# P times V for eight key tiles behind every second block, the down projection behind the others

## The chip, the cores and the metric

The kernel runs on one core of one Trainium2 chip. The metric is the device time of one execution in microseconds (us), the median of several runs. The core has five engines with queues of their own: TensorE (PE, its weight loads are listed as PEld), VectorE (DVE), ScalarE (ACT), GpSimd (POOL) and SyncE (SP, which here only issues DMAs). Each works through its queue in order and waits there for semaphores of the others.

## The reference

One sequence of S = 2048 rows with D = 576 features, H = 32 heads of 18, F = 4608. All in float32.

```python
xn = layernorm(x)
# attention
q, k, v = split(xn @ wqkv)                       # 32 heads of 18
p = softmax(q @ k.T * 18 ** -0.5)                # full, 2048 x 2048 for each head
s = concat(p @ v) @ wo
# gated block
gate, up = xn @ W_gate, xn @ W_up                # 2048 x 4608
b = (gate * (gate > 0) * up) @ W_down
out = x + s * silu(b)
```

## The kernel before, in words

A first stage (to about 200 us) makes the normalised rows, their transpose, and q, k, v. The main stage is a sequence of **144 blocks**, k = 0 to 143: 4 groups of 512 rows of x, and in each 36 tiles of 128 of the 4608 features. `up(k)` multiplies one such feature tile (gate on PE rows 0 to 63, up on rows 64 to 127, two matmuls side by side), three products each since every operand is held as a high and a low part. `emit_unit(k)` (from L868) writes a block. Into its 27 pairs of gate and up matmuls (`pg`) it deals two kinds of attention matmuls, which use the same half arrays:

- `psx`, the scores of 128 keys against 512 queries, whose exponential ACT writes to a buffer `p` (L97, tile from the pool `pp`: one buffer holds one key tile for two heads and 1024 queries);
- `pm`, scores whose row maxima DVE takes (L272) for the next pair of heads.

From block 16 on, each of the 16 pairs of heads takes eight blocks: 16 `psx` and 16 `pm` in each block, so four key tiles. I call this stretch of a block its **row run**. Behind it, before the change, stand

- `attend()`, P times V: for each finished key tile four matmuls of 32 columns side by side (`po`; the chip shows two instructions for each float32 matmul). After 16 key tiles `finish` has ACT evict the result (`ot`) and leaves a task `rest_` for DVE: transpose (`tq`), reciprocal (`rc`), scaling, transpose back (`on`);
- in even blocks the tasks (`run_tasks`: `rest_` and `max_rows`, which collects the maxima with a reduction and a transpose, `nm` and `nt`) and then `down(k - 1)`, the down projection of two feature tiles: eight results `py` of six matmuls each, each added to the rows `y` by DVE (L725).

Scores, maxima and `py` share one pool of PSUM banks, `psS` with five buffers used in turn (`shared(...)`), so the result that is made as the fifth after another waits until that one has been read. All matmuls, all DVE operations and all of POOL's (`vec`, `gp`) stay in the order in which they are written.

`gate_step` turns one finished tile of 128 rows of `y` into silu: ACT writes a tanh to `e` (one buffer, L736), POOL scales `e` and multiplies `y` by it, and POOL sends `y` to DRAM. It is called once in a block, at the ninth pair of the row run, while a group's four tiles are waiting. POOL also splits raw weights into high and low parts (`split_up`: `gw` from `rg`; `split_down`: `dw` from `rd`).

## Time and profile before

| what | us |
|---|---|
| median of 3 runs (2610.35 to 2611.09) | 2610.72 |
| the profiled execution's own time | 2611.43 |
| its span, first to last instruction | 2609.7 |
| PE busy, DVE busy | 2590.9, 1900.1 |
| ACT busy, POOL busy | 1383.3, 1197.8 |

The span and what lies around it (1.7 us) make up the profiled execution's time, which is 0.7 us over the median. In the timeline, a row is a start, a length, the engine, the line, the operation with its tiles, and a count where equal neighbours were merged; in brackets stands how long the engine had been idle and what released it.

### The profile page before, as it was taken

The numbers are of one execution on the slowest core, as the hardware profiler recorded it, in microseconds if no ns is written. First come the engines' busy times: TensorE is split into PE (matmuls) and PEld (weight loads), VectorE is DVE, ScalarE is ACT, GpSimd is POOL, SyncE is SP. The second block draws the span as 40 slices with busy tenths as digits, with TensorE's granted clock in tenths as the row PEclk, the third lists the DMA queues.
The fourth block names the chain that finished last, engine by engine and source line by source line (L and its number), as shares of the span: only waits on it lengthen the run. The fifth ranks groups of instructions, "written<-read, shape, count | busy, mean of one in ns | idle before, by whom it ended". The sixth has DMA issues, their size and how long they took to land.

```text
span 2609.7 us, 54494 instructions
## 1 busy us (share of the span) xinstructions
PE 2590.9 (99%) x21788; PEld 2035.6 (78%) x21788; DVE 1900.1 (73%) x3145; ACT 1383.3 (53%) x2594; POOL 1197.8 (46%) x971
## 2 busy tenths in 40 slices
PE   8999999999999999999999999999999999999999
PEld 7898887777777777777777777777777777777778
DVE  5335678788878788787887787887777878778235
ACT  2321135556665556555666555555556655555642
POOL 5246764344464434443455444444346444434554
PEclk9999999999999999999999999999999999999999
DMA  7867422222542322232363222222253232222245
GB/s 246 274 211 162 104 74 69 70 73 74 116 121 57 82 65 70 58 79 64 80 150 88 67 69 72 65 73 68 71 128 105 73 75 60 76 58 62 67 121 183
DMA packets 263806, 253.11 MB, mean 97 GB/s; under 512 B 27648, under 2 KB 208896, under 8 KB 263552
## 3 DMA queue, kind: packets, MB, share of 16 engines
q1 hardware_dynamic: 255808, 222.48, 32.9%
q0 software_dynamic: 7744, 27.14, 3.1%
q8 instruction: 172, 2.82, 0.5%
q14 instruction: 82, 0.67, 0.1%
HBM read 203.01 MB, written 46.01 MB: 95 GB/s over the span
## 4 chain that ended last, share of the span: by engine, by line
PE 97%; DMA 1%; POOL 1%; DVE 1%; issue 0%; ACT 0%; SPq 0%; POOLq 0%; DVEq 0%; ACTq 0%
PE pg L68 32%; PE po L68 19%; PE py L68 18%; PE pm L68 11%; PE psx L68 9%; PE pq L68 4%; PE pv L68 2%; PE pw L68 2%; DMA rg<-in_B_W_up_dram 0%; PE tps L76 0%; POOL wv L85 0%; DMA xt<-in_A_x_dram 0%; DMA ro<-od 0%; SPq L97 0%; DMA y<-gd 0%
## 5 line engine op out<-in xcount | busy, mean ns | idle before, releaser
L272 DVE TENSOR_REDUCE mx<-pm 128x1 f32<-128x512 f32 x2048 | 1363.9, 689 | 268.8 <-PE pm L68 148.9
L97 ACT ACTIVATE p<-psx 128x512 f32<-128x512 f32 x2048 | 1097.9, 603 | 583.0 <-PE psx L68 541.5
L68 PE MATMUL pg<-x,gw 64*128 64x512 f32 x7560 | 1372.8, 394 | 2.3 <-POOL gw L85 1.8
L68 PEld LDWEIGHTS pg<-x,gw 64*128 64x128 f32 x7560 | 1033.5, 186 | 85.9 <-issue 3.7
L85 POOL TENSOR_TENSOR hh<-h,hh 128x512 fp32r<-128x512 f32 x144 | 184.3, 1280 | 812.7 <-ACT hh L97 790.7
L68 PEld LDWEIGHTS py<-dw,hh 128*128 128x128 f32 x3456 | 460.1, 188 | 56.1 <-issue 31.8
L68 PE MATMUL py<-dw,hh 128*128 128x288 f32 x3456 | 476.8, 297 | 0.0
L68 PE MATMUL po<-p,va 128*32 128x512 f32 x4096 | 465.9, 595 | 0.0
L725 DVE TENSOR_TENSOR y<-py,y 128x288 f32<-128x288 f32 x544 | 244.3, 454 | 225.9 <-PE py L68 225.8
L85 POOL TENSOR_TENSOR gw<-rg,gw 128x1152 fp32r<-128x1152 f32 x144 | 385.9, 2680 | 11.6
L68 PEld LDWEIGHTS po<-p,va 128*32 128x32 f32 x4096 | 119.8, 109 | 276.2 <-issue 265.4
L85 POOL CAST dw<-rd 128x576 fp32r<-128x576 f32 x144 | 95.8, 665 | 387.7 <-PE py L68 382.1
L68 PE MATMUL psx<-qT,kq 56*128 56x512 f32 x608 | 229.8, 392 | 0.0
L68 PE MATMUL pm<-kq,qT 54*128 54x512 f32 x608 | 228.7, 398 | 0.1
L85 POOL TENSOR_TENSOR dw<-rd,dw 128x576 fp32r<-128x576 f32 x144 | 206.3, 1433 | 11.6
L97 ACT ACTIVATE hh<-h 128x512 fp32r<-128x512 f32 x144 | 90.8, 630 | 220.7 <-DVE h L696 220.7
L68 PE MATMUL psx<-kq,kA 56*128 56x512 f32 x512 | 195.4, 393 | 0.3 <-DVE h L696 0.2
L68 PE MATMUL pm<-kq 54*128 54x512 f32 x512 | 195.3, 402 | 0.0
L68 PE MATMUL psx<-kq 56*128 56x512 f32 x512 | 194.2, 392 | 0.0
L68 PE MATMUL pm<-kA,kq 54*128 54x512 f32 x512 | 193.6, 400 | 0.1
L85 POOL CAST gw<-rg 128x1152 fp32r<-128x1152 f32 x144 | 165.4, 1149 | 0.0
L68 PE MATMUL pm<-kA,qT 54*128 54x512 f32 x416 | 159.4, 402 | 0.0
(92 smaller groups left out, 2180.5 us busy)
## 6 DMA issues: line engine op xcount, KB each, us to landing
rg<-in_B_W_gate_dram SPq DMA_DIRECT2D x144, 288.0 KB
rg<-in_B_W_up_dram SPq DMA_DIRECT2D x144, 288.0 KB
rd<-in_B_W_down_dram SPq DMA_DIRECT2D x144, 288.0 KB
x<-xTd SPq DMA_DIRECT2D x72, 256.0 KB
qd<-hh POOLq DMA_DIRECT2D x16, 512.0 KB, 5.0
kd<-hh POOLq DMA_DIRECT2D x16, 512.0 KB, 6.1
xTd<-x SPq DMA_DIRECT2D x16, 512.0 KB
kq<-kd SPq DMA_DIRECT2D x210, 36.0 KB
```

Source lines behind the costliest of these rows:

```text
L68: return tc.keep_in_program_order(nc.tensor.matmul(*args, **kw))
L85: return lambda *args, **kw: tc.keep_in_program_order(op(*args, **kw))
L97: i = op(*args, **kw)
L272: vec(nc.vector.tensor_reduce(mx[:, h, b, j, c : c + 1], ps, axis=AX.X, op=ALU.max))
L725: vec(nc.vector.tensor_tensor(ys[j][:, cs], ps, ys[j][:, cs], ALU.add))
```

## The change

The row run stays. Behind an odd block now stand all eight key tiles of two blocks, and behind an even block the down projection alone. `max_rows` runs behind each block in which it falls due (these are odd ones), `rest_` from a list of its own (`outs`) in the even blocks, ahead of the down projection. For eight buffers `p`, memory comes from seven places: one buffer of raw weights (`wr`) in place of two, blocks 2 to 15 borrow `p` buffers for theirs; `hh` has three buffers in place of four and `h` one in place of two, with the ReLU written into it; `yp` five in place of six; the buffer of the last output weights and those of the last stage's rows are taken from `wr` and from a weight buffer; DMA scratch shrinks. `gate_step` is called twice in a block, at pairs 9 and 25.

```diff
-    wr = pool(early, "wr", 2)
+    wr = pool(early, "wr", 1)
...
     def load_up(k):
         if k < len(units):
             f = units[k][1]
-            rgs[k] = wr.tile([P, KC, P], F32, name="rg")
+            if 1 < k < N1:
+                rgs[k] = as_rg(pp.tile([P, 4, 512], F32, name="p"))
+            else:
+                rgs[k] = wr.tile([P, KC, P], F32, name="rg")
...
-    pp = pool(mid, "pp", 4, "right")
-    w4 = pool(mid, "w4", 1, "right")
+    pp = pool(mid, "pp", 8, "right")
     wl = pool(mid, "wl", 2, "right")
-    yp = pool(mid, "yp", 6, "right")
+    yp = pool(mid, "yp", 5, "right")
...
-        r = hp.tile([P, 512], F32, name="r", bufs=1)
-        ac.activation(r, ps[0], AF.Relu)
-        h = hp.tile([P, 512], F32, name="h")
-        vec(nc.vector.tensor_tensor(h, ps[1], r, ALU.mult))
-        hh = hp.tile([P, 2, 512], F32R, name="hh", bufs=4)
+        h = hp.tile([P, 512], F32, name="h", bufs=1)
+        ac.activation(h, ps[0], AF.Relu)
+        vec(nc.vector.tensor_tensor(h, ps[1], h, ALU.mult))
+        hh = hp.tile([P, 2, 512], F32R, name="hh", bufs=3)
...
-        tasks.append((rest_, ()))
+        outs.append((rest_, ()))
...
     def emit_unit(k, ex, ns, mx, nm):
         if k - 1 in rds:
             split_down(k - 1)
+        if k == len(units) - 2:
+            split_up(k + 1)
+            out_weights(4)
...
-            if i == 8:
+            if i in (8, 24):
                 gate_step()
         up_end(k, ps)
-        while ready:
-            attend()
-        if k % 2 == 0 and k:
-            run_tasks()
+        run_tasks(tasks)
+        if k % 2:
+            while ready:
+                attend()
+        elif k:
+            run_tasks(outs)
             down(k - 1)
...
                 if i == 6:
+                    gx = ws.tile([P, 2, KC, P], F32, tag="gw", name="gx").rearrange("p a c s -> p (a c s)")
+                    sy = [gx[:, j * D : (j + 1) * D] for j in range(2)]
+                    sx = [gx[:, (2 + j) * D : (3 + j) * D] for j in range(2)]
...
                     for j in range(4):
                         project(j, *inputs.pop(j))
+                        rows_of(j + 2, sy[j % 2], sx[j % 2])
+                        inputs[j + 2] = *split_heads(j + 2, spare[j % 2]), sy[j % 2], sx[j % 2]
...
-    nc = _bacc.Bacc("TRN2", target_bir_lowering=False, num_devices=1)
+    nc = _bacc.Bacc("TRN2", target_bir_lowering=False, num_devices=1, dynamic_dma_scratch_size=4096)
```

On DVE, two blocks of which the second (an even one) follows the end of 16 key tiles stood in this order before (`mx` maxima of `pm`, `h` gate times up, then `max_rows`, `rest_`, and the eight additions of `py`):

```order
L272 TENSOR_REDUCE mx<-pm 128x1 x16
L696 TENSOR_TENSOR h<-pg_5586,r 128x512
L272 TENSOR_REDUCE mx<-pm 128x1 x16
L696 TENSOR_TENSOR h<-pg_5775,r 128x512
L769 TENSOR_REDUCE nm_2842<-mx 128x16
L775 STREAM_TRANSPOSE nt<-nm_2842 128x32
L803 STREAM_TRANSPOSE tq<-ot 128x512
L806 RECIPROCAL rc<-tq 128x16
L808 TENSOR_TENSOR tq<-tq,rc 128x16x18
L813 STREAM_TRANSPOSE on<-tq 128x512
L725 TENSOR_TENSOR y<-py,y 128x288 x8
```

The same two blocks in the changed kernel:

```order
L272 TENSOR_REDUCE mx<-pm 128x1 x16
L700 TENSOR_TENSOR h<-pg_5548,h 128x512
L775 TENSOR_REDUCE nm_2839<-mx 128x16
L781 STREAM_TRANSPOSE nt<-nm_2839 128x32
L272 TENSOR_REDUCE mx<-pm 128x1 x16
L700 TENSOR_TENSOR h<-pg_5766,h 128x512
L809 STREAM_TRANSPOSE tq<-ot 128x512
L812 RECIPROCAL rc<-tq 128x16
L814 TENSOR_TENSOR tq<-tq,rc 128x16x18
L819 STREAM_TRANSPOSE on<-tq 128x512
L729 TENSOR_TENSOR y<-py,y 128x288 x8
```

The two steps of `max_rows` have moved into the odd block; the four of `rest_` still stand between `h` and the additions of the even block.

On ACT, the first two blocks after a group's end, before (`e` is the tanh of `gate_step`, `p` the exponentials, `r` the ReLU):

```order
L97 ACTIVATE p<-psx 128x512 x4
L736 ACTIVATE e<-y 128x576
L97 ACTIVATE p<-psx 128x512 x12
L97 ACTIVATE r<-pg_9841 128x512
L97 ACTIVATE hh<-h 128x512
L97 ACTIVATE p<-psx 128x512 x4
L736 ACTIVATE e<-y 128x576
```

and in the changed kernel:

```order
L97 ACTIVATE p<-psx 128x512 x4
L740 ACTIVATE e<-y 128x576
L97 ACTIVATE p<-psx 128x512 x6
L740 ACTIVATE e<-y 128x576
L97 ACTIVATE p<-psx 128x512 x6
L97 ACTIVATE h<-pg_9784 128x512
L97 ACTIVATE hh<-h 128x512
L97 ACTIVATE p<-psx 128x512 x4
L740 ACTIVATE e<-y 128x576
```

A second tanh has come in between the tenth and the eleventh exponential of the same block.

## The prediction

> **What bounds the kernel now.** I read the page's busy times first, then its chain of waits, then timelines of two neighbouring blocks.

> ```profile
> span 2609.7 us, 54494 instructions
> PE 2590.9 (99%) x21788; PEld 2035.6 (78%) x21788; DVE 1900.1 (73%) x3145; ACT 1383.3 (53%) x2594; POOL 1197.8 (46%) x971
> PE 97%; DMA 1%; POOL 1%; DVE 1%; issue 0%; ACT 0%; SPq 0%; POOLq 0%; DVEq 0%; ACTq 0%
> L68 PE MATMUL po<-p,va 128*32 128x512 f32 x4096 | 465.9, 595 | 0.0
> ```

> PE is busy 99% of the span and makes 97% of the chain; no other engine is ever what it waits for, beyond some microseconds in all. So the time is the sum of PE's runs, and only two things can move it: a shorter run, or a wait that is new. The last row counts the P times V instructions: 4096, in runs of 32 so 128 runs, one for each block from 16 to 143.

> ```profile
> 1204.13 0.49 PE L68 MATMUL pm<-kq,qT 54*128 54x512 f32 x1
> 1214.41 3.64 PE L68 MATMUL po<-p,va 128*32 128x512 f32 x32
> 1214.87 0.13 PEld L68 LDWEIGHTS po<-p,va 128*32 128x32 f32 x4 [0.30 <-issue]
> 1215.30 0.13 PEld L68 LDWEIGHTS po<-p,va 128*32 128x32 f32 x4 [0.30 <-issue]
> 1217.98 0.49 PE L68 MATMUL pm<-kq,qT 54*128 54x512 f32 x1
> 1228.21 3.64 PE L68 MATMUL po<-p,va 128*32 128x512 f32 x32
> 1231.79 6.61 PE L68 MATMUL py<-dw,hh 128*128 128x288 f32 x48
> 1238.33 0.49 PE L68 MATMUL pm<-kq,qT 54*128 54x512 f32 x1
> ```

> Two blocks take 34.20 us (1204.13 to 1238.33): a row run of 10.28, P times V 3.57, a row run of 10.23, P times V 3.58, down projection 6.54, each from its own start to the start of the next.

> **The change: what it saves.** The two P times V runs become one of 64 instructions. Inside a run a group of four instructions follows the last after 0.43 us (1214.87 to 1215.30), eight groups in a run. So the long run takes 3.57 + 8 x 0.43 = 7.01 us, where the two took 7.15: the entry and exit of one run fall away, 0.14 us. There are 64 such pairs: **-9.0 us**, between -7.7 and -10.2 for 0.12 to 0.16. I assume that a row run passes to a down projection at the price at which it passes to P times V; every other matmul is the same.

> **What it uncovers.** In an even block the P times V run stood between the row run and the down projection. DVE used it. This is an even block after the end of 16 key tiles (PE's two rows first, then DVE):

> ```profile
> 1194.01 3.64 PE L68 MATMUL po<-p,va 128*32 128x512 f32 x32
> 1197.58 6.62 PE L68 MATMUL py<-dw,hh 128*128 128x288 f32 x48
> ...
> 1190.84 4.70 DVE L272 TENSOR_REDUCE mx<-pm 128x1 f32<-128x512 f32 x7 [0.30 <-PE pm L68]
> 1195.46 0.68 DVE L696 TENSOR_TENSOR h<-pg,r 128x512 f32<-128x512 f32 x1
> 1196.05 0.21 DVE L769 TENSOR_REDUCE nm<-mx 128x16 f32<-128x64 f32 x1
> 1196.47 0.71 DVE L803 STREAM_TRANSPOSE tq<-ot 128x512 f32<-128x512 f32 x1
> 1198.51 0.71 DVE L813 STREAM_TRANSPOSE on<-tq 128x512 f32<-128x512 f32 x1
> 1199.15 0.79 DVE L725 TENSOR_TENSOR y<-py,y 128x288 f32<-128x288 f32 x2
> 1200.27 0.46 DVE L725 TENSOR_TENSOR y<-py,y 128x288 f32<-128x288 f32 x1 [0.34 <-PE py L68]
> 1204.24 0.46 DVE L725 TENSOR_TENSOR y<-py,y 128x288 f32<-128x288 f32 x1 [0.33 <-PE py L68]
> ```

> The row run ends at 1194.01 (call it R). DVE is 1.45 us behind with the maxima, takes `h`, `max_rows`, then `rest_` from 1196.47, and begins the first addition to `y` at 1199.15. Of the change's edits only `max_rows` leaves this place: 1196.05 to 1196.47, 0.42 us. So in the new kernel the first addition begins at R + 5.14 - 0.42 = 4.72 and ends 0.46 later, at R + 5.18. How soon PE moves on after DVE is seen where it does wait, behind two additions of the last stage:

> ```profile
> 2543.39 0.82 DVE L955 TENSOR_TENSOR y<-pw,y 128x288 f32<-128x288 f32 x2 [2.36 <-DMA y<-gd]
> 2543.90 0.85 PE L68 MATMUL psx<-qT,kA 56*128 56x512 f32 x2 [0.80 <-DVE y L955]
> ```

> The first of the two ends at 2543.39 + 0.46 = 2543.85, so 0.05 us. Now PE's side: with P times V gone, the down projection begins at R, and its eight results use five banks. The sixth needs the bank of the first, so the end of that first addition. Undisturbed it would begin after five eighths of 6.54 us, at R + 4.09. It can begin at R + 5.23: **1.14 us late**, and what stands behind it on PE's queue (the seventh, the eighth, the next row run) is late by as much. The seventh waits no more: its addition ends 0.4 us later, the matmuls 0.8. Before, the sixth was due at R + 3.57 + 4.09 and nothing showed. In even blocks without `rest_` the first addition ends about 2.7 us earlier, at R + 2.5: no wait there.

> How many: results end twice for each of 16 pairs of heads; those of the last pair run elsewhere (behind the odd block 139, and at the end), so 30 blocks. 30 x 1.14 = **+34.2 us**. Bounds: DVE's work between R and the next row run, from the windows of this block:

> ```profile
> 1194.00:1197.60 3.60, 3.60 (x34) 0.95 (x33) 3.50 (x9) 1.09 (x2) 0.72 (x1) 1.00 0.00 0
> 1197.60:1204.20 6.60, 6.60 (x54) 6.43 (x50) 4.58 (x9) 0.00 (x0) 0.89 (x2) 1.00 0.10 25
> ```

> The columns after the length are PE, PEld, DVE. DVE is busy 3.50 + 4.58 = 8.08 us; without `max_rows` 7.66 must fit into 6.54 and the 0.57 by which the last addition overhangs already (1204.24 + 0.46 against 1204.13). At the very least 0.55 us: +16.5. Upward I add 0.1 for PE's new start after a wait: +37.2. I take 34, since the banks decide before the sum does.

> **The second tanh.** `gate_step` now comes twice in each of the two blocks after a group's end (three groups; the fourth's tiles go elsewhere), where four blocks had one each. `e` is one buffer, and ACT takes its queue in order: the second tanh, and all exponentials behind it, wait until POOL has used the first. The first block after a group's end, an odd one, before:

> ```profile
> 724.56 0.50 PE L68 MATMUL pm<-kq,qT 54*128 54x512 f32 x1
> 732.37 0.39 PE L68 MATMUL psx<-kq,kA 56*128 56x512 f32 x1
> 735.02 0.64 PE L68 MATMUL po<-p,va 128*32 128x512 f32 x4
> ...
> 727.50 0.70 ACT L736 ACTIVATE e<-y 128x576 f32<-128x576 f32 x1
> 728.08 6.49 ACT L97 ACTIVATE p<-psx 128x512 f32<-128x512 f32 x12
> ...
> 724.30 0.66 POOL L85 CAST dw<-rd 128x576 fp32r<-128x576 f32 x1 [5.70 <-PE py L68]
> 727.65 2.68 POOL L85 TENSOR_TENSOR gw<-rg,gw 128x1152 fp32r<-128x1152 f32 x1
> 730.29 0.20 POOL L85 CAST nr<-nt 128x32 fp32r<-128x32 f32 x1
> 730.77 0.66 POOL L85 CAST dw<-rd 128x576 fp32r<-128x576 f32 x1
> 733.67 1.43 POOL L85 TENSOR_TENSOR y<-y,e 128x576 f32<-128x576 f32 x1
> ```

> The first tanh runs at 727.50, but POOL, held until the down projection has freed `dw` (724.30), works through two splits of `dw` and one of `gw` first and reads `e` last until 735.10, 10.54 us into the block. `max_rows`' split `nr` (730.29 to 730.77) leaves this block, so 10.06. The second tanh stands at pair 25, due at 25 x 0.24 = 6.0 us, and waits until 10.1. It takes 0.70, the eleventh exponential behind it (6.49 / 12 =) 0.54: 11.35. The fourteenth `psx`, five tiles after the eleventh, needs that bank and was due at 732.37, 7.81 us in: 3.5 us late, some 0.3 more while ACT catches up. In the even block POOL is free (its `gw` split is done behind the 7 us run), and a second tanh costs there what one costs before: this row run took 10.46 where the others take 10.24, 0.22. Per group: 3.8 + 0.2, less 0.4 for two later blocks without a tanh: 3.6; **+11 us** for three. Bounds: 0 if POOL comes early after all, 15 if ACT catches up slowly.

> **What I cost at nothing.** `max_rows` (0.42 us of DVE) and its small DMAs move an odd block's P times V ahead: hidden by 7 us without DVE work, and needed a block later than written. `h` in place with one buffer: POOL reads it about 4 us after a row run's end, the next ReLU comes 10 us later or more; without that cover 0.6 us each. `hh` and `yp`: a tile is wanted when the one before has been read for 10 us. The single `wr`: the rival below. First blocks and last stage: the same chains of store and reload; I allow -1 to +5.

> Sum: -9 + 34 + 11 = **+36** on the profiled execution's 2611.4, so 2647.4; the median of the runs is 0.7 lower, so **2647**.

> [...] Before, PE stood 1.84 us here, and the clock stayed whole (the figure after the engines):

> ```profile
> 217.03 0.73 PE L68 MATMUL pg<-x,gw 64*128 64x512 f32 x4 [1.84 <-POOL gw L85]
> 214.00:218.00 4.00, 2.16 (x18) 1.52 (x16) 2.00 (x4) 1.23 (x2) 2.89 (x2) 1.00 1.11 202
> ```

> [...]

> **Rivals.**

> 1. *Only the saving*: DVE is in time. It needs the first addition 1.14 us earlier, so a DVE less behind at R, or `rest_` after the additions, and a POOL in time too. The order on DVE is fixed and shows `rest_` ahead; the backlog of 1.45 us comes from 16 maxima in a row run, which stay. Time 2610.7 - 9 = **2602**. Chance 0.06.
> 2. *One of the two waits alone*, or waits that just cancel the saving: without the tanh 2636, inside my range; near zero 0.03.
> 3. *Weights late*: with one `wr`, the load for block k + 2 starts only when POOL has split that of k + 1. In the odd block above that split is over at 730.3, 5.8 us in. A load behind a busy queue took 5 us:

> ```profile
> 2536.93 0.40 SPq L97 DMA_DIRECT2D ro<-od  x1
> 2541.89 0.63 ACT L97 ACTIVATE x<-ro 128x512 fp32r<-128x512 f32 x1 [4.09 <-DMA ro<-od]
> ```

> Two of them: at 16, split at 20, wanted at 34. SP's queue stands behind that wait, with the loads of heads, which are written a pair of heads ahead. It would decide from 14 us of delay on; each microsecond beyond costs 64 us, so **2700 and more**. Chance 0.04.

> **How the numbers follow.** My forecast, both waits or nearly so: 0.87. Range: both waits at their lower bounds, 2611 - 9 + 16 + 0 = 2618, I hold unlikely together; one low and the other as counted gives 2629 and 2636. Upward 37 + 15 + 5 - 8 gives 2660. I say **2628 to 2660**. A difference under 0.2% (5.2 us) can't be told from none. Faster 0.06, same 0.03, slower 0.91.

> **What would show it.** P times V in 64 runs of 64 instructions, 7.0 us each; waits of PE at the sixth `py` for DVE's `y`, 30 of some 1.1 us, and none in other even blocks; three waits of PE at a `psx` for ACT of 3 to 4 us, and a tanh released by POOL. Wrong: even blocks with `rest_` no longer than the others, a row run that waits for `gw` in many blocks, or first and last stages that move by more than 5 us.

## The result, and the profile after

| | median us | runs, from to |
|---|---|---|
| before | 2610.89 | 2610.35 to 2611.23 |
| after | 2672.63 | 2671.78 to 2673.21 |

The ratio is 1.0237, with a 95% interval of 1.0223 to 1.025: 62 us slower. The forecast was slower, 2647, with a range up to 2660. The sign and both named waits were right; the size was 25.6 us too small, and the time lies 12.6 us above the range.

The page of the changed kernel, its span, busy times and chain of waits:

```profile
span 2670.8 us, 54049 instructions
PE 2598.4 (97%) x21788; PEld 2050.7 (77%) x21788; DVE 1900.2 (71%) x3145; ACT 1383.6 (52%) x2594; POOL 1199.2 (45%) x971
PE 88%; DVE 6%; DMA 2%; POOL 2%; issue 1%; ACT 1%; SPq 0%; DVEq 0%; POOLq 0%; ACTq 0%
L68 PE MATMUL py<-dw,hh 128*128 128x288 f32 x3456 | 484.6, 298 | 41.4 <-DVE y L729 41.4
```

DVE had 1% of the chain and now has 6%. The last row gives the largest single sum: PE stood 41.4 us in front of `py` for DVE's additions to `y`. Here is one such block (PE, then DVE and POOL), from the timeline:

```profile
1150.66 4.23 PE L68 MATMUL py<-dw,hh 128*128 128x288 f32 x30
1156.31 1.86 PE L68 MATMUL py<-dw,hh 128*128 128x288 f32 x12 [1.41 <-DVE y L729]
...
1152.14 0.68 DVE L700 TENSOR_TENSOR h<-pg,h 128x512 f32<-128x512 f32 x1
1152.73 0.70 DVE L809 STREAM_TRANSPOSE tq<-ot 128x512 f32<-128x512 f32 x1
1153.56 1.29 POOL L85 TENSOR_TENSOR hh<-h,hh 128x512 fp32r<-128x512 f32 x1 [10.94 <-ACT hh L97]
1153.76 1.41 DVE L814 TENSOR_TENSOR tq<-tq,rc 128x288 f32<-128x288 f32 x1
1155.20 0.71 DVE L819 STREAM_TRANSPOSE on<-tq 128x512 f32<-128x512 f32 x1
```

Thirty matmuls make five results, then PE waits for the bank of the first. DVE takes `rest_` in between, and its scaling (L814) takes 1.41 us where it took 0.97 before. The second wait, in the first block after a group's end (ACT, POOL, PE), and PE's clock there:

```profile
736.72 0.70 ACT L740 ACTIVATE e<-y 128x576 f32<-128x576 f32 x1
742.40 1.40 POOL L85 TENSOR_TENSOR y<-y,e 128x576 f32<-128x576 f32 x1
743.83 0.68 ACT L740 ACTIVATE e<-y 128x576 f32<-128x576 f32 x1 [3.30 <-POOL y L85]
745.05 0.79 PE L68 MATMUL psx<-kq,kA 56*128 56x512 f32 x1 [3.29 <-ACT p L97]
```
```profile
740.00:742.00 2.00, 1.76 (x16) 1.15 (x12) 1.68 (x4) 0.53 (x1) 1.92 (x3) 1.00 0.30 87
744.00:746.00 2.00, 0.95 (x4) 0.95 (x6) 0.00 (x0) 2.00 (x5) 1.78 (x3) 0.50 1.07 342
748.00:750.00 2.00, 2.00 (x10) 1.27 (x7) 1.05 (x3) 1.19 (x2) 0.00 (x0) 0.50 1.02 311
750.00:752.00 2.00, 2.00 (x17) 0.56 (x20) 1.77 (x3) 0.20 (x2) 0.00 (x0) 0.80 0.94 270
```

In the windows the figure after the five engines' busy times is the granted clock. It is 0.50 from PE's new start until about 750.8. And at the beginning of the main stage something that the prediction costed at nothing (POOL, then PE):

```profile
210.32 1.97 POOL L85 MEMSET va<- 128x832 f32 x6 [8.21 <-DMA vd<-ev]
216.89 2.62 POOL L85 TENSOR_TENSOR gw<-p,gw 128x1152 fp32r<-128x1152 f32 x1
216.87 0.73 PE L68 MATMUL pg<-x,gw 64*128 64x512 f32 x4 [2.66 <-POOL gw L85]
219.57 2.07 PE L68 MATMUL pg<-x,gw 64*128 64x512 f32 x8 [1.97 <-POOL gw L85]
```

To put numbers on the parts I lined up the starts of the 72 down projections in the two traces; the growth of the difference from one to the next belongs to the blocks between them. A wait is counted as the distance of two matmuls less the usual one.

| part | forecast | after less before, us |
|---|---|---|
| shorter P times V | -9 | -8.9 (64 x 0.139) |
| 30 waits at the sixth `py` | +34 | +46.3 |
| three group changes, beside their wait at `py` | +12 | +17.9 (6.25, 6.48, 5.17) |
| one gate fewer in two later blocks, three times | -1 | -2.0 |
| up to the first down projection | 0 | +5.1 |
| left over in all other blocks and at the end | 0 | +2.8 |
| sum | +36 | +61.2 |

The last but one row fits PE's new start behind each of 30 waits, for which I had 0.1 us in the bound and nothing in the sum: in the trace of the changed kernel PE takes 2.58 us (median) from its first matmul behind a wait, the 31st of the 48, to the next row run, and 2.47 in the blocks without a wait.

### The profile page after: what moved, and what is told of

The parts are those of the page before. It is cut to its first block, busy times and chain, and to the rows that moved or that the text cites. A ratio compares the mean times of both kernels' runs of the same rounds, so it can differ in the third digit from the quotient of the medians.

```text
span 2670.8 us, 54049 instructions
## 1 busy us (share of the span) xinstructions
PE 2598.4 (97%) x21788; PEld 2050.7 (77%) x21788; DVE 1900.2 (71%) x3145; ACT 1383.6 (52%) x2594; POOL 1199.2 (45%) x971
## 4 chain that ended last, share of the span: by engine, by line
PE 88%; DVE 6%; DMA 2%; POOL 2%; issue 1%; ACT 1%; SPq 0%; DVEq 0%; POOLq 0%; ACTq 0%
PE pg L68 30%; PE po L68 17%; PE py L68 14%; PE pm L68 10%; PE psx L68 9%; PE pq L68 4%; PE pv L68 2%; PE pw L68 2%; DVE tq L814 2%; DVE mx L272 1%; DVE on L819 1%; DVE tq L809 1%; DVE h L700 1%; DMA x<-xTd 1%; POOL dw L85 0%
## 5 line engine op out<-in xcount | busy, mean ns | idle before, releaser
L272 DVE TENSOR_REDUCE mx<-pm 128x1 f32<-128x512 f32 x2048 | 1367.0, 690 | 469.2 <-PE pm L68 287.9
L68 PE MATMUL pg<-x,gw 64*128 64x512 f32 x7560 | 1379.6, 396 | 5.3 <-POOL gw L85 4.6
L97 ACT ACTIVATE p<-psx 128x512 f32<-128x512 f32 x2048 | 1098.0, 603 | 532.0 <-PE psx L68 485.6
L68 PEld LDWEIGHTS pg<-x,gw 64*128 64x128 f32 x7560 | 1038.1, 188 | 89.3 <-POOL gw L85 5.5
L85 POOL TENSOR_TENSOR hh<-h,hh 128x512 fp32r<-128x512 f32 x144 | 184.9, 1284 | 1030.0 <-ACT hh L97 993.4
L68 PE MATMUL py<-dw,hh 128*128 128x288 f32 x3456 | 484.6, 298 | 41.4 <-DVE y L729 41.4
L68 PEld LDWEIGHTS py<-dw,hh 128*128 128x128 f32 x3456 | 460.8, 188 | 74.0 <-DVE y L729 48.4
L68 PE MATMUL po<-p,va 128*32 128x512 f32 x4096 | 453.7, 595 | 0.0
L85 POOL TENSOR_TENSOR gw<-rg,gw 128x1152 fp32r<-128x1152 f32 x130 | 346.8, 2668 | 10.4
L68 PEld LDWEIGHTS po<-p,va 128*32 128x32 f32 x4096 | 126.7, 110 | 292.8 <-issue 281.6
L729 DVE TENSOR_TENSOR y<-py,y 128x288 f32<-128x288 f32 x544 | 227.6, 449 | 77.2 <-PE py L68 73.1
L68 PE MATMUL psx<-qT,kq 56*128 56x512 f32 x608 | 232.5, 394 | 3.3 <-ACT p L97 3.3
L68 PE MATMUL pm<-kq,qT 54*128 54x512 f32 x608 | 228.7, 399 | 0.4 <-DVE mx L272 0.4
L85 POOL TENSOR_TENSOR dw<-rd,dw 128x576 fp32r<-128x576 f32 x144 | 206.4, 1434 | 11.5
L97 ACT ACTIVATE hh<-h 128x512 fp32r<-128x512 f32 x144 | 90.9, 631 | 213.3 <-DVE h L700 213.3
L68 PE MATMUL psx<-kq,kA 56*128 56x512 f32 x512 | 196.3, 395 | 3.5 <-ACT p L97 3.3
L68 PE MATMUL psx<-kq 56*128 56x512 f32 x512 | 195.4, 393 | 0.0
L68 PE MATMUL pm<-kq 54*128 54x512 f32 x512 | 195.3, 403 | 0.0
L68 PE MATMUL pm<-kA,kq 54*128 54x512 f32 x512 | 193.8, 402 | 0.2 <-DVE mx L272 0.2
L85 POOL CAST dw<-rd 128x576 fp32r<-128x576 f32 x144 | 95.5, 663 | 213.4 <-PE py L68 206.3
L68 PE MATMUL psx<-qT,kA 56*128 56x512 f32 x416 | 158.6, 395 | 3.5 <-ACT p L97 3.3
L68 PE MATMUL pm<-kA,qT 54*128 54x512 f32 x416 | 159.5, 403 | 0.0
```

The lines of the kernel that those rows point to most:

```text
L68: return tc.keep_in_program_order(nc.tensor.matmul(*args, **kw))
L85: return lambda *args, **kw: tc.keep_in_program_order(op(*args, **kw))
L97: i = op(*args, **kw)
L272: vec(nc.vector.tensor_reduce(mx[:, h, b, j, c : c + 1], ps, axis=AX.X, op=ALU.max))
L729: vec(nc.vector.tensor_tensor(ys[j][:, cs], ps, ys[j][:, cs], ALU.add))
```

## The experiments

All are the changed kernel with one edit, unless said otherwise. The theory: three independent causes, DVE's `rest_` in front of the additions, the second tanh with a fall of the clock, and POOL's wait for `ev`. The rival is that fewer buffers (banks, one `wr`, `h`, `hh`) cost the time, wherever the waits show.

**`rest_` behind odd blocks.**

```diff
         if k % 2:
+            run_tasks(outs)
             while ready:
                 attend()
         elif k:
-            run_tasks(outs)
             down(k - 1)
```

> rest_ runs behind odd blocks, ahead of the 7 us of P times V, no longer ahead of the down projection. Theory (DVE's rest_ holds the bank that the sixth py needs, 30 times some 1.55 us in the changed kernel's trace): the 30 waits at py vanish, 46 us less, 2626. Rival (the five banks or the missing 3.6 us of cover in itself, since down now follows the row run at once): waits at py stay in all or most blocks, under 10 us gained. In between (by my own forecast of 1.14 us each): 34 us less, 2638.

Measured 2623.49 us, ratio 1.0049 (1.0034 to 1.0064): 49.1 us less. The group of `py`, of this kernel:

```profile
L68 PE MATMUL py<-dw,hh 128*128 128x288 f32 x3456 | 476.8, 297 | 0.0
```

All 30 waits are gone, with the same five banks and the down projection still right behind the row run. So five banks do not make them by themselves; where `rest_` stands in DVE's queue decides. The 3 us beyond the 46.3 were not traced to a cause; new starts of PE and scatter between executions would fit. The scaling still takes 1.39 us here (median), beside 7 us of P times V, and costs nothing.

**Why 1.55 us a wait and not 1.14: `rest_` ahead of `h`.** In even blocks `run_tasks(outs)` moves from behind `up_end` to ahead of it.

> In even blocks DVE takes rest_ ahead of h instead of behind it; nothing else moves. In the changed kernel the scaling tq (L814) takes 1.41 us while POOL subtracts h from hh; it took 0.46 where POOL did nothing. Theory (DVE's scaling is held up by POOL's subtraction): the scaling takes 0.46 again, the 30 waits at py fall from 1.55 to some 0.65 us, 27 us less, 2646. Rival (the scaling is long whatever runs beside it, or PE's writes slow it): it stays at 1.4, the waits stay, 2672.

Measured 2643.14 us, ratio 1.0125 (1.0108 to 1.0142): 29.5 less. An even block of it (DVE, PE, POOL):

```profile
1140.22 0.46 DVE L814 TENSOR_TENSOR tq<-tq,rc 128x288 f32<-128x288 f32 x1
1141.35 0.65 DVE L700 TENSOR_TENSOR h<-pg,h 128x512 f32<-128x512 f32 x1
1142.41 2.65 PE L68 MATMUL py<-dw,hh 128*128 128x288 f32 x18 [0.48 <-DVE y L729]
1142.74 1.30 POOL L85 TENSOR_TENSOR hh<-h,hh 128x512 fp32r<-128x512 f32 x1 [13.02 <-ACT hh L97]
```

The scaling takes 0.46 us once POOL's subtraction no longer runs beside it, and the wait falls from 1.41 to 0.48. The group's sum of idle time is 13.2 us in place of 41.4. DVE has the same operations to do before the first addition; what has changed is their order, and so what runs beside what. The scaling is 0.95 us shorter, and the wait 0.93. The row of before that I should have read with the prediction's others, POOL's subtraction and the scaling in an even block:

```profile
1196.88 1.28 POOL L85 TENSOR_TENSOR hh<-h,hh 128x512 fp32r<-128x512 f32 x1 [8.69 <-ACT hh L97]
1197.51 0.97 DVE L808 TENSOR_TENSOR tq<-tq,rc 128x288 f32<-128x288 f32 x1
```

Before, the scaling ended 1198.48, 0.32 us after POOL (1198.16). After, it ends 1155.17, again 0.32 after POOL (1154.85), although it began 0.20 and not 0.63 us behind POOL's start. So the scaling's end followed POOL's end and not its own start. POOL's subtraction is released by `h`, and `max_rows` stood behind `h`: moving `max_rows` out brought the scaling forward by 0.40 us and made it 0.44 longer. All 30 scalings of this kind in the trace of the changed kernel end 0.31 to 0.32 us after POOL, and so do the 30 of before; the one of before with no operation of POOL beside it (at 2479.09) takes 0.46 us. What in the chip ties the two was not shown. The three lengths agree with it: 1.09 us that POOL still had to go at the scaling's start and 0.32 make 1.41, 0.65 and 0.32 make 0.97, and with nothing beside it the scaling takes 0.46. The additions to `y`, with one input in PSUM, keep their 0.45 us: in the changed kernel 218 of the 544 run beside an operation of POOL, none over 0.46.

**The second gate leaves odd blocks.**

```diff
-            if i in (8, 24):
+            if i == 8 or (i == 24 and k % 2 == 0):
```

> The second gate_step of a block stays in even blocks and leaves odd ones: three tiles in the first two blocks after a group's end, the fourth in the next. Theory (the second tanh waits for the one e buffer, and the gap it makes brings the clock down): the three group changes, which cost 7.8, 8.1 and 6.8 us in the changed kernel, give 19 to 22 us back, 2651 to 2653, and the clock stays at 1.00 after them. Rival (the time goes to weights or rows that come late with one wr buffer, or to five y buffers): no change, 2672.

Measured 2657.48 us, ratio 1.0177 (1.0162 to 1.0192): 15.2 less. In its trace the three group changes cost 0.09, 0.09 and 0.13 us beside the wait at `py`, so the second tanh explains them, and 17.6 us of the 17.9 are back. My number was too hopeful for two reasons: I had counted the waits at `py` that lie in these blocks (1.5 each) into them, and the first stage of this profile came out 1.6 us later.

**The wait or the clock: the second gate later.** In odd blocks it moves from pair 25 to pair 33, and in another run, of a single execution, to pair 29.

> In odd blocks the second gate_step moves from pair 25 to pair 33, 1.9 us later in the row run, with the same end of POOL's use of e. So PE's gap should fall from 3.3 to some 1.4 us. Theory (a gap of over 3 us costs half the clock for some 5 us, about as much again as the wait): the clock stays at 1.00, a group change costs 1.5 to 2.5 us where it cost 6.8 to 8.1, 16 to 18 us less, 2655. Rival (the time beyond the wait is ACT catching up with its exponentials): only the wait shrinks, 6 us less, 2667.

> The second gate_step of odd blocks at pair 29, between the changed kernel (pair 25: PE's gap 3.3 us, the clock fell) and the run with pair 33 (1.0 us, clock whole). PE's gap should be some 2.2 us, in one piece. If one idle stretch has to be over some 3 us, the clock stays at 1.00 and a group change costs some 2.7 us beside the wait at py; if 2 us are enough, the clock falls to half again and it costs 5.

Pair 33: 2658.83 us, ratio 1.0184 (1.0169 to 1.0199), 13.8 less. Pair 29: one execution with a span of 2664.2, against 2670.8. PE's wait and the windows around it, of pair 33 first, then of pair 29:

```profile
745.62 0.50 PE L68 MATMUL pm<-kA,qT 54*128 54x512 f32 x2 [0.97 <-ACT p L97]
744.00:746.00 2.00, 1.03 (x7) 0.37 (x3) 1.03 (x2) 1.60 (x4) 1.66 (x3) 1.00 1.08 283
746.00:748.00 2.00, 2.00 (x22) 0.68 (x24) 1.85 (x3) 0.54 (x2) 1.62 (x3) 1.00 1.07 261
```
```profile
744.68 0.50 PE L68 MATMUL pm<-kq,qT 54*128 54x512 f32 x1 [2.10 <-ACT p L97]
744.00:746.00 2.00, 1.32 (x11) 1.07 (x12) 0.75 (x2) 2.00 (x5) 1.88 (x3) 0.96 1.05 337
746.00:748.00 2.00, 2.00 (x12) 0.40 (x12) 1.98 (x4) 0.69 (x2) 1.19 (x2) 0.50 1.00 210
748.00:750.00 2.00, 2.00 (x16) 0.51 (x12) 0.54 (x1) 0.63 (x1) 0.70 (x1) 0.68 1.07 324
```

| second gate in odd blocks | PE's wait at the three group changes, us | clock at 0.50 for | cost, us |
|---|---|---|---|
| pair 25 | 3.29, 3.27, 3.27 | 6.8, 6.8, 3.4 us | 6.25, 6.48, 5.17 |
| pair 29 | 2.10, 2.09, 2.14 | 3.4, 3.4 us, not at all | 4.12, 4.03, 2.56 |
| pair 33 | 0.97, 0.98, 1.03 | not at all | 1.39, 1.39, 1.43 |

At the first group change the wait shrinks by 2.3 us from pair 25 to 33 and the cost by 4.9: the other 2.5 are the clock. ACT catching up, the rival, would have left them. At pair 29 a wait of 2.1 us was enough for the clock to fall at two of three group changes, so my condition "over some 3 us" is wrong for this kernel. At the third the clock stayed whole behind the longest of the three waits, and the cost is 1.5 us lower; the last section shows why.

**POOL's zeroing later.** The memsets of `va` and `nm` move from ahead of block 0 to behind block 2.

> The zeroing of va and nm on POOL moves from ahead of block 0 to behind block 2. Theory (POOL stood 8.2 us at it for the DMA out of ev, the weights of block 2 came late, PE stood twice some 3 us and the clock fell to half): 5 to 6 us less, 2667, first py where it was before the change, no window of 6 us between 214 and 232 under 0.95 of the clock. Rival (the weights of block 2 are late because the one wr or the borrowed p buffers load late): the gaps stay, under 1 us gained.

Measured 2669.93 us, ratio 1.0231 (1.0214 to 1.0248): 2.7 less (though one of its four runs took 2674.2), half of what I expected, and the clock still fell (windows of 2 us from 218: 0.73, 0.50, 0.92). What was left, in its trace (POOL, PE):

```profile
213.81 1.14 POOL L85 CAST gw<-p 128x1152 fp32r<-128x1152 f32 x1 [0.56 <-DMA p<-in_B_W_up_dram]
215.01 0.73 PE L68 MATMUL pg<-x,gw 64*128 64x512 f32 x4 [0.67 <-POOL gw L85]
217.72 1.20 PE L68 MATMUL pg<-x,gw 64*128 64x512 f32 x8 [1.97 <-POOL gw L85]
```

The wait for `ev` is gone. What is left is a gap of 0.67 us for the weights of block 2, whose load is issued 1.0 us later than before (202.59 against 201.63). But the 2.7 us are not the price of the wait for `ev` alone: the clock is at half for 3.4 us here and for 6.8 in the changed kernel's trace. Three of these kernels (`rest_` ahead of `h`, pair 29, and P times V behind each block, below) keep the memsets and have 3.4 us of half clock here. From the first gate and up matmul to the first down projection they take 3.7 to 4.1 us more than the kernel before, this one 2.6 and the changed kernel 5.6. By these traces the wait for `ev` itself is worth 1.1 to 1.5 us, and the rest is the clock.

**All memory as changed, but P times V behind each block.** `attend()` runs in every block again, `rest_` between it and the down projection.

> All memory as changed and two gates, but P times V stands behind every block again, for four key tiles, and rest_ between it and the down projection. Theory: no saving and no waits at py; the first blocks (5.1) and the three group changes (19) are left over the kernel before, 2634 to 2637. If the fewer buffers (h, hh, wr) were part of the 46 us of waits at py, these would show here too: up to 2680.

Measured 2644.53 us, ratio 1.0128 (1.0113 to 1.0143), 7.5 us over the range that I expected. No wait at `py` is left, so fewer buffers by themselves do not make those. But at each group's end there is a wait that neither kernel shows (SP's queue, then PE):

```profile
695.98 0.47 SPq L97 DMA_DIRECT2D x<-xTd  x1
699.41 0.60 SPq L97 DMA_DIRECT2D rg<-in_B_W_gate_dram  x1
700.74 11.62 SPq L97 DMA_DIRECT2D x<-xTd  x13
...
718.53 0.49 PE L68 MATMUL pg<-x,gw 64*128 64x512 f32 x1 [1.00 <-DMA x<-xTd]
```

SP holds the load of the next weights until the one `wr` is free, and the rows `x` of the next group stand behind it; PE waits four times for them at the first group's end. This block costs 6.0, 6.1 and 4.1 us more than before at the three ends. It is the rival "weights late" in a small form. The 7 us run that the pairing puts there hides it: in the changed kernel this row run begins 10.1 us after SP's 13 loads of `x` (704.48), here 6.6 after 700.74.

**The three edits together, and then the weights of block 2 first.** In the second kernel their load goes ahead of that of block 0's down weights, and POOL splits them ahead of those.

> The three edits together. If the three causes are all there is, what is left of the change is the shorter P times V: the profiled time of before less 8.9 us, so 2600 to 2603, 0.3% under the kernel before. If they are not independent, or the pairing costs something that no row shows, between 2606 and 2625.

> The kernel with the three edits together, and in the first blocks the weights of block 2 go first: they are loaded ahead of the down weights of block 0 and split ahead of them on POOL. Theory (what was left of the first blocks' 5 us, 2.7, comes from these weights: their load landed 0.7 us late, PE had two gaps of 0.7 and 2.0 us and the clock fell): the weights are ready some 2 us earlier, one gap or none, the clock stays, 2 to 3 us less than with the three edits, 2602. Rival (the loads share a full DMA, so the order changes nothing): 2605.

Three edits: 2605.09 us, ratio 0.9976 (0.9967 to 0.9985), 2 us over what I expected. With the weights first: 2604.34 us, ratio 0.9969 (0.9957 to 0.9982). The two times can't be told apart, so they do not decide what the order of the weights is worth, and both beat both kernels: the shorter P times V is real, some 6 us of it after what the first blocks still cost. The chain of the first of the two reads like that of before:

```profile
PE 97%; DMA 1%; POOL 1%; issue 0%; DVE 0%; SPq 0%; ACT 0%; POOLq 0%; DVEq 0%; ACTq 0%
```

In the trace of the second, the stretch from the first gate and up matmul to the first down projection is 1.8 us longer than before, where with the three edits alone it is 2.7. The gap of 0.7 us is gone; one gap is left there, much like that of before (1.84), but with the clock behind it:

```profile
217.49 1.58 PE L68 MATMUL pg<-x,gw 64*128 64x512 f32 x8 [1.98 <-POOL gw L85]
218.00:220.00 2.00, 2.00 (x12) 1.58 (x12) 0.47 (x1) 0.00 (x0) 1.45 (x2) 0.53 0.00 0
```

## Why the prediction was right or wrong

1. **What bounds the kernel.** Right: PE's runs add up, and all but some 2 us of what was lost is a wait of PE at one of three places, or the half clock behind it.
2. **The saving.** Right: -0.139 us a pair, as forecast (-0.14), and nothing else in the pairing costs time.
3. **The wait at the sixth `py`.** The mechanism, the count (30) and the even blocks without a wait were right; the size was off. The step that failed is "ends at R + 5.14 - 0.42": I let all DVE work after `max_rows` move up by its 0.42 us. The scaling could not, since its end is tied to POOL's subtraction (0.31 to 0.32 us behind it, 30 times), which is tied to `h`. Without the 0.42 the same sum gives 1.56 us; the waits were 1.53 to 1.59, but for one of 1.0. My upper bound, 37.2, took each duration from before as fixed and so did not hold either. Of the 25 us that the sum lacked, 12 are this step, 6 are under 4 and 5 under 5.
4. **The second tanh.** The wait was right (forecast 3.5 at the fourteenth `psx`, measured 3.3 idle there). The size was off by the clock, which is not in the sum: behind the one gap of before that the prediction shows, 1.84 us, it had stayed whole. Each of the three waits of 3.3 us brought one or two periods of half clock (6.83, 6.83 and 3.41 us at 0.50), in which PE lost 2.9, 3.1 and 1.7 us (half of its busy time in them).
5. **Costed at nothing.** Right for `h`, `hh`, `yp`, `max_rows` and the last stage. Wrong for the first blocks: I followed who waits for the tiles that lost a buffer, and not who takes over the memory of those that moved. `ev` lay in `hh`'s buffers; the change gives it buffers of its own (an edit that the excerpt ahead of the prediction leaves out), and `va`, made later, waits 8.2 us for `ev`'s DMAs, which it did not before. With the weights of block 2 and the half clock behind the gaps that makes 5.1 us, just beyond the +5 that I allowed.
6. **Rivals.** "Only the saving" is what the kernel with three edits shows, once the waits are away. "Weights late" is real, at 4 to 6 us a place and not 64 for each microsecond, and shows only without the long run.

## What to carry to other kernels

Before work is moved up on an engine, ask of each operation behind it what fixes its end: here the scaling was fixed by POOL, and the room that `max_rows` left was lost. Two runs of work that wait for each other's buffers are best separated by work that needs neither, as P times V did for `rest_` and the down projection; when such cover moves, move the work that it covered with it. And a stall of PE of the size of these, 1.98 to 3.3 us, is to be priced with half clock behind it: in these traces 1.5 to 3.1 us beside the stall, but for the one of 2.14 us that the end of a clock period cut into 0.87 and 1.27 (last section).

## What the hardware showed that I had not expected

```profile
742.45:745.86 3.41, 1.31 (x11) 1.01 (x12) 1.05 (x2) 2.40 (x5) 2.98 (x4) 1.00 1.13 285
745.86:749.27 3.41, 3.41 (x22) 0.78 (x22) 2.63 (x5) 1.46 (x3) 1.33 (x2) 0.50 1.03 240
2010.06 0.49 PE L68 MATMUL pm<-kq 54*128 54x512 f32 x1 [2.14 <-ACT p L97]
2005.38:2008.79 3.41, 2.54 (x21) 1.72 (x19) 2.35 (x4) 1.12 (x3) 3.33 (x3) 1.00 0.83 178
2008.79:2012.21 3.42, 2.15 (x20) 1.31 (x24) 1.58 (x3) 3.23 (x6) 2.73 (x4) 1.00 0.95 296
2012.21:2015.62 3.41, 3.41 (x40) 1.02 (x36) 1.60 (x3) 0.63 (x1) 1.65 (x2) 1.00 0.31 116
```

  The first wait lies in one period, which is idle for 2.10 us. The third is cut in two by the end of a period, 0.87 and 1.27 us idle, and the 1.84 of before likewise (1.37 and 0.47). Over all eleven traces, from the first whole clock on, each of the 35 periods with 1.79 us or more of idle time was followed by a fall, and none with up to 1.60; of two in between (1.74 and 1.75) one was. In the changed kernel the four ahead of the falls were idle for 2.68, 2.23, 2.73 and 3.18 us, and no other at whole clock, up to 2660 us, for more than 1.43. So in these traces it was a matter of where a wait of some 2 us fell whether it cost the clock.
- **An operation of DVE, the scaling, trebled beside POOL's subtraction**, from 0.46 to 1.41 us, with no change to itself.
